# One fetch per set of weights, into the place of its decoded halves; first loads ahead of a branch

## The chip, the cores and the metric

The kernel runs on one core of a Trainium2 chip. The metric is the device time of one launch in microseconds; the median of three runs is taken.

## What is computed

A linear attention with decay is followed by two feed-forward layers. The inputs of the attention are float32; the four weight arrays of the layers are float64 and reach the kernel as their 8-byte words.

```python
state = zeros(B, H, D, D)                       # B 4, H 8, S 768, D 48
for t in range(S):
    cur   = (u * k[t]) outer v[t]
    y[t]  = r[t] @ (state + cur)
    state = w * state + k[t] outer v[t]
x = y as (3072 tokens, 384)
x = max(h, 0.01 * h) @ w_out    with h = x @ w_in     # 384 -> 2048 -> 384
x = (h * cos(h)) @ w_out2       with h = x @ w_in2
```

## The kernel before, in words

The attention is cut into 24 units of 128 tokens (u = 0 to 23, two chunks of 64 tokens each). A unit has three pieces. `prep` (lines 279 to 292) scales its keys, receptances and bonus on VectorE. `piece_a` (line 303) makes the scores `pa` and the state's update `pu` on TensorE, writes the bonus into the diagonal with eight ScalarE copies (line 321), and merges the scores on VectorE (line 322). `piece_y` (`piece_y1` for the first eight units) makes the output `py` on TensorE, copies it out as `yo` on ScalarE (line 371, one buffer), and GpSimd's queue writes it to the DRAM tensor `xt` (line 374). `load_xu` then reads the unit back from `xt` with its rows over partitions, as a quarter of a token block's input `xl` (line 441), and `split_xu` splits it into a rounded high part `xh` (ScalarE, line 445) and the rest `xl` (VectorE, line 446).

The feed-forward layers run over 12 blocks of 512 tokens (0 to 5 for the first layer, 6 to 11 for the second) and, in each, over 16 groups f of 128 hidden columns: a slot (j, f). A slot has nine matmuls for the hidden values (`g1`, line 458: high by low, low by high, high by high, three each), a step on ScalarE and VectorE that applies the nonlinearity and splits the result again (`evac_a`, `evac_b`, lines 463 to 487), and nine matmuls into the block's output (`g2`, lines 498 to 500) two slots later. The slots begin with (0, 0) to (0, 7); then block 0 and block 1 alternate: (0, 8), (1, 0), (0, 9), (1, 1) and so on. Block 0 needs units 0 to 3, block 1 needs units 4 to 7. The pieces of units 4 to 7 are put among the first slots by `due`.

The weights of each f are decoded on the chip from the 8-byte words into a high half `wh` and a low half `wl` (`split_w`, line 256). `load_w` (line 246) fetches the set twice: the words as they are (`wr`), and shifted by two bytes (`wo`), which puts the middle bits of each word into one 32-bit place. Each has two buffers, and so a fetch waits for a decode two sets earlier. A decode has two ScalarE instructions (the sign, line 266; the exponent, line 269) and five on VectorE (lines 267, 270, 271, 273, 275). The tiles `wh10` to `wh15` and `wl10` to `wl15` are first lent to units 0 to 7 (`lent`, line 83) for their inputs and states.

All loads go through SP's queue in the order in which the program lists them, and SP issues them one after the other: one that waits for a buffer holds up all behind it. `load(u)` has five DMAs (lines 112 to 120; keys, receptances, a natural-order copy of r and k, two of v), 1,024 KB together. A branch on the size of the decays (line 189) stands ahead of the loads of unit 1 and later; the path behind it for other decays isn't taken with these inputs. After the branch, the list `first` sets the order on ScalarE and of the loads: `p`, `a` and `y` are pieces of units, `d` a decode, `l` a unit's load. The other engines' orders are made by a planner with a model of the times. For layer 2, sets 0 to 4 have tiles of their own, and set f from 5 on takes the tiles of layer 1's set f - 5 (line 259).

## Time and profile before

| | us |
|---|---|
| median of 3 runs | 957.91 |
| lowest, highest | 955.81, 962.46 |
| span of the profiled execution, first to last instruction | 954.9 |
| TensorE busy with matmuls in the span | 896.4 (94%) |
| VectorE busy | 647.5 (68%) |
| ScalarE busy | 521.7 (55%) |
| bytes moved by DMA | 99.79 MB, of which 84.59 MB read from device memory |

The page of the profile gives the profiled execution's own time as this span; what lies around it in a timed run is the difference to the runs. Busy shares are means over the whole span; the stages differ, and the stages are read from the timelines.

### The profile page before, as it was taken

The numbers are of one execution on the slowest core, as the hardware profiler recorded it, in microseconds if no ns is written. First come the engines' busy times: TensorE is split into PE (matmuls) and PEld (weight loads), VectorE is DVE, ScalarE is ACT, GpSimd is POOL, SyncE is SP. The second block draws the span as 40 slices with busy tenths as digits, with TensorE's granted clock in tenths as the row PEclk, the third lists the DMA queues.
The fourth block names the chain that finished last, engine by engine and source line by source line (L and its number), as shares of the span: only waits on it lengthen the run. The fifth ranks groups of instructions, "written<-read, shape, count | busy, mean of one in ns | idle before, by whom it ended". The sixth has DMA issues, their size and how long they took to land.

```text
span 954.9 us, 15397 instructions
## 1 busy us (share of the span) xinstructions
PE 896.4 (94%) x5954; PEld 734.8 (77%) x5954; DVE 647.5 (68%) x1072; ACT 521.7 (55%) x1050; POOL 53.1 (6%) x92
## 2 busy tenths in 40 slices
PE   1648979999999999999999999999999999999997
PEld 1646858887778888878888788888888888888886
DVE  7768979449865776675848877565665755665654
ACT  1435545635654564563645566665665655665654
POOL 3111100000100000001000000000000000000000
PEclk9957989999999999999999999999999999999999
DMA  7579786024512322252828910100100100100000
GB/s 191 160 248 310 257 287 187 1 68 131 174 47 65 114 98 89 95 204 74 306 69 276 314 72 1 33 34 1 34 34 1 62 4 9 59 1 0 34 1 34
DMA packets 41277, 99.79 MB, mean 104 GB/s; under 512 B 4976, under 2 KB 8176, under 8 KB 41200
## 3 DMA queue, kind: packets, MB, share of 16 engines
q1 hardware_dynamic: 31552, 75.96, 24.6%
q0 software_dynamic: 4896, 14.16, 4.7%
q10 hardware_dynamic: 4752, 8.65, 2.4%
q8 instruction: 47, 0.77, 0.3%
q14 instruction: 30, 0.25, 0.1%
HBM read 84.59 MB, written 14.16 MB: 103 GB/s over the span
## 4 chain that ended last, share of the span: by engine, by line
PE 75%; DMA 10%; DVE 8%; ACT 3%; issue 2%; SPq 0%; POOL 0%; POOLq 0%; ACTq 0%; DVEq 0%
PE ph L458 35%; PE po L498 12%; PE po L499 12%; PE po L500 12%; DMA wr<-in_wmoe 2%; DMA xl<-xt 2%; PE pa L309 2%; PE py L346 2%; ACT ar L321 1%; DMA natt<-in_nat 1%; DMA xt<-yo 1%; PE pu L316 1%; DVE wh L270 1%; DVE wl L275 1%; DMA wo<-in_wmoe 1%
## 5 line engine op out<-in xcount | busy, mean ns | idle before, releaser
L498 PE MATMUL po<-gh,wl 128*128 128x512 f32 x576 | 228.0, 396 | 2.9 <-ACT gh L485 2.7
L499 PE MATMUL po<-gh,wh 128*128 128x512 f32 x576 | 224.6, 390 | 0.0
L500 PE MATMUL po<-gl,wh 128*128 128x512 f32 x576 | 207.0, 391 | 0.7 <-DVE gl L486 0.7
L486 DVE TENSOR_TENSOR gl<-ga,gh 128x512 fp32r<-128x512 f32 x192 | 132.2, 689 | 94.7 <-ACT gh L485 80.6
L485 ACT CAST gh<-ga 128x512 fp32r<-128x512 f32 x192 | 118.6, 619 | 120.1 <-PE po L499 73.3
L458 PE MATMUL ph<-xl,wh 128*128 128x512 f32 x576 | 169.1, 396 | 5.9 <-DVE xl L446 4.8
L458 PE MATMUL ph<-xh,wh 128*128 128x512 f32 x576 | 168.1, 391 | 0.0
L458 PE MATMUL ph<-xh,wl 128*128 128x512 f32 x576 | 165.0, 392 | 0.0
L458 PEld LDWEIGHTS ph<-xl,wh 128*128 128x128 f32 x576 | 108.2, 190 | 30.7 <-DVE xl L446 5.2
L498 PEld LDWEIGHTS po<-gh,wl 128*128 128x128 f32 x576 | 108.1, 188 | 28.0 <-ACT gh L485 4.1
L458 PEld LDWEIGHTS ph<-xh,wl 128*128 128x128 f32 x576 | 109.0, 189 | 23.1
L500 PEld LDWEIGHTS po<-gl,wh 128*128 128x128 f32 x576 | 107.9, 188 | 24.4 <-DVE gl L486 1.8
L458 PEld LDWEIGHTS ph<-xh,wh 128*128 128x128 f32 x576 | 109.0, 189 | 23.0
L499 PEld LDWEIGHTS po<-gh,wh 128*128 128x128 f32 x576 | 108.2, 188 | 21.4
L321 ACT ACTIVATE ar<-ident,bon 64x64 f32<-64x64 f32 (+1 forms) x320 | 80.7, 333 | 26.6 <-DVE bon L290 26.3
L473 DVE SCALAR_TENSOR_TENSOR gt<-gt,ga 128x512 f32<-128x512 f32 x96 | 65.8, 689 | 38.9 <-ACT gt L472 38.4
L468 DVE TENSOR_TENSOR ga<-ph,ga 128x512 f32<-128x512 f32 x96 | 66.0, 688 | 37.8 <-ACT ga L467 37.4
L478 DVE TENSOR_TENSOR ga<-ph,gt 128x512 f32<-128x512 f32 x96 | 65.8, 689 | 36.3 <-ACT gt L477 35.7
L467 ACT ACTIVATE ga<-ph 128x512 f32<-128x512 f32 x96 | 57.1, 594 | 59.2 <-PE ph L458 56.1
L477 ACT ACTIVATE gt<-gt 128x512 f32<-128x512 f32 x96 | 59.8, 627 | 49.8 <-DVE gt L475 49.7
L471 ACT ACTIVATE ga<-ph 128x512 f32<-128x512 f32 x96 | 57.4, 598 | 44.3 <-PE ph L458 30.3
L472 ACT ACTIVATE gt<-ga 128x512 f32<-128x512 f32 x96 | 60.2, 631 | 1.6
(128 smaller groups left out, 754.0 us busy)
## 6 DMA issues: line engine op xcount, KB each, us to landing
wr<-in_wmoe SPq DMA_DIRECT2D x32, 768.0 KB, 6.0
wo<-in_wmoe SPq DMA_DIRECT2D x32, 767.5 KB, 5.7
natt<-in_nat SPq DMA_DIRECT2D x20, 384.0 KB, 4.1
xt<-yo POOLq DMA_DIRECT2D x48, 96.0 KB, 3.6
x2t<-ob ACTq DMA_DIRECT2D x18, 256.0 KB, 2.0
xl<-x2t POOLq DMA_DIRECT2D x6, 768.0 KB, 4.7
kst<-in_ks SPq DMA_DIRECT2D x20, 224.0 KB, 3.4
vs<-in_nat SPq DMA_DIRECT2D x40, 96.0 KB, 4.1
```

The costliest lines, as they stand in the source:

```text
L321: nc.scalar.activation(out=ar[q, c, g], in_=ident2[q], func=AF.Copy, scale=bon[q, g:g + 1])
L458: nc.tensor.matmul(out=p, lhsT=w_[:, 0, k * 128:(k + 1) * 128], rhs=x_[:, k], start=(m == 0), stop=(m == 3 * KT - 1))
L468: nc.vector.tensor_tensor(out=ga, in0=p, in1=ga, op=ALU.max)
L472: nc.scalar.activation(out=gt, in_=ga, func=AF.Copy, bias=MAGIC)
L473: nc.vector.scalar_tensor_tensor(out=gt, in0=gt, scalar=MAGIC, in1=ga, op0=ALU.subtract, op1=ALU.subtract)
L477: nc.scalar.activation(out=gt, in_=gt, func=AF.Sin, scale=-TWOPI)
L478: nc.vector.tensor_tensor(out=ga, in0=p, in1=gt, op=ALU.mult)
L485: nc.scalar.copy(out=gh, in_=ga)
L486: nc.vector.tensor_tensor(out=gl, in0=ga, in1=gh.bitcast(F32), op=ALU.subtract)
L498: nc.tensor.matmul(out=o, lhsT=w_l[:, 1, sl], rhs=gh, start=(f == 0), stop=False)
L499: nc.tensor.matmul(out=o, lhsT=w_h[:, 1, sl], rhs=gh, start=False, stop=False)
L500: nc.tensor.matmul(out=o, lhsT=w_h[:, 1, sl], rhs=gl, start=False, stop=(f == NF - 1))
```

## The change

Each set of weights is fetched once, into a tile that has the size of its two decoded halves and is their place afterwards (tag `w0` to `w15`, and `w16` to `w20` for layer 2's first five). The shifted copy goes; in its place the decode puts the two 16-bit parts of the middle bits side by side in a small tile `mid`: one by a ScalarE copy, the other by VectorE's `and`, now on 16-bit elements. The sign, the masked word and `mid` have tiles of their own (two buffers each). ScalarE has three instructions in a decode, VectorE five.

Since a raw set waits for no decode, the loads are listed anew: ahead of the branch come the loads of units 0 to 3, `uu`, and the sets 0 to 3; sets 4 to 9 and units 4 to 7 stand in `first` (`w` is the fetch of a set); sets 10 to 15, whose places are lent, are fetched after unit 7's `piece_y`. SP's queue is in program order from the start of the kernel.

```diff
--- before.py
+++ after.py
@@ -40,6 +40,7 @@
 HOLD = 16
 AHEAD = 1
 LOADS = 2
+LENT = 10
 EXTRA = 5
 FIRST = 3
 ONE = 8
@@ -48,7 +49,6 @@
 QY = 'gpsimd'
 QO = 'scalar'
 QX = 'gpsimd'
-WRB = 2
 KSB = 2
 NATB = 2
 YOB = 1
@@ -81,11 +81,14 @@
     vs_ = [ap_.tile([128, 2, H, D], F32, name=f"vs{i}") for i in range(2)]
 
     def lent(i, *shape):
-        t = wp.tile([128, 768], F32, tag=i, name=f"lent_{i}")
+        if i[2:] not in lent_:
+            lent_[i[2:]] = wp.tile([128, 2, 768], F32, tag=f"w{i[2:]}", name=f"lent_{i[2:]}")
+        t = lent_[i[2:]]
         n = shape[1] * (shape[2] if len(shape) > 2 else 1)
-        t = t[0:shape[0], 0:n]
+        t = t[0:shape[0], int(i[1] == "l"), 0:n]
         return t.rearrange("p (a b) -> p a b", a=shape[1]) if len(shape) > 2 else t
 
+    lent_ = {}
     ss_ = [lent(i, 128, 768).rearrange("t (c h d) -> t c h d", c=2, h=H) for i in ("wh15", "wl15", "wh10")]
     rf_ = [t[0:PACK, 1] for t in ar_] + [lent(i, PACK, H, HC) for i in ("wh14", "wl14")]
     kf_ = [ap_.tile([PACK, H, HC], F32, tag="ks", bufs=KSB, name="kst") for i in range(2)]
@@ -122,8 +125,28 @@
 
 
     wt = const.tile([PACK, H], F32, name="wt")
+    ub = ap_.tile([128, H, D], F32, name="ub")
+    wh, wl, wraw = {}, {}, {}
+
+    def set_of(L, f):
+        return (wp, f) if L == 0 else (rest[0], NF + f) if f < EXTRA else (wp, f - EXTRA)
+
+    def load_w(L, f):
+        pool, i = set_of(L, f)
+        t = wraw[L, f] = pool.tile([128, 2, 384, 2], I32, tag=f"w{i}", name=f"raw{i}")
+        nc.sync.dma_start(
+            out=t.rearrange("p z a b -> p z (a b)"), in_=wmoe[L, f].bitcast(I32).rearrange("z p c -> p z c"))
+
+    ctx.enter_context(tc.manual_schedule(engines={mybir.EngineType.SP}))
     nc.sync.dma_start(out=wt, in_=wT)
     load(0)
+    nc.sync.dma_start(out=ub, in_=uu)
+    load(1)
+    load(2)
+    load_w(0, 0)
+    load(3)
+    for i in range(1, 4):
+        load_w(0, i)
     w2 = const.tile([PACK, H], F32, name="w2")
     ws = const.tile([PACK, H], F32, name="ws")
     nc.vector.memset(ws, 1.0)
@@ -179,8 +202,6 @@
                 out=ps[TOK[c], i], lhsT=(pw[HALF[0], i] if c else pt[HALF[1], 1, i]),
                 rhs=ident[ROWS[c], ROWS[c]], start=True, stop=True)
     nc.scalar.copy(out=kn, in_=ps)
-    ub = ap_.tile([128, H, D], F32, name="ub")
-    nc.sync.dma_start(out=ub, in_=uu)
     sm = ap_.tile([D, H, D], F32, name="sm")
 
     slow = nc.values_load(flag[0:1, 0:1], min_val=0, max_val=1)
@@ -194,8 +215,8 @@
             t = mp.tile([128, 512], F32, tag=n, bufs=2, name=n)
             return t[:, 0:shape[0] * shape[1]].rearrange("p (a b) -> p a b", a=shape[0])
 
-        buf = [wp.tile([128, 2, 384, 2], I32, tag="wr", bufs=WRB, name="wr") for _ in range(2)]
-        buf = [t.rearrange("p z a b -> p (z a b)").bitcast(F32) for t in buf]
+        buf = [wp.tile([128, 2, 384], I32, tag="dt", bufs=2, name="dt") for _ in range(2)]
+        buf = [t.rearrange("p z a -> p (z a)").bitcast(F32) for t in buf]
         st, cu = [t[:, 0:D * E].rearrange("p (d e) -> p d e", d=D) for t in buf]
         wv, uv = [buf[0][:, D * (E + i):D * (E + i + 1)] for i in range(2)]
         uk = buf[1][:, D * E:D * (E + 1)]
@@ -241,37 +262,26 @@
 
     rebias = const.tile([128, 1], F32, name="rebias")
     nc.vector.memset(rebias, REBIAS)
-    wh, wl, wraw = {}, {}, {}
-
-    def load_w(L, f):
-        t = wp.tile([128, 2, 384, 2], I32, tag="wr", bufs=WRB, name="wr")
-        nc.sync.dma_start(
-            out=t.rearrange("p z a b -> p z (a b)"), in_=wmoe[L, f].bitcast(I32).rearrange("z p c -> p z c"))
-        s = wp.tile([128, 2, 4 * 384], U16, tag="wo", bufs=WRB, name="wo")
-        nc.sync.dma_start(
-            out=s[:, :, 0:4 * 384 - 1],
-            in_=wmoe[L, f].bitcast(U16).rearrange("z p c -> p z c")[:, :, 1:4 * 384])
-        wraw[L, f] = t, s
-
     def split_w(L, f):
-        t, o = wraw.pop((L, f))
-
-        pool, i = (wp, f) if L == 0 else (rest[0], NF + f) if f < EXTRA else (wp, f - EXTRA)
-        h = wh[L, f] = pool.tile([128, 2, 384], F32R, tag=f"wh{i}", name=f"wh{i}")
-        l = wl[L, f] = pool.tile([128, 2, 384], F32R, tag=f"wl{i}", name=f"wl{i}")
+        t = wraw.pop((L, f))
         top = t[:, :, :, 1]
-        mid = o.bitcast(I32).rearrange("p z (c i) -> p z c i", i=2)[:, :, :, 0]
-        s = t[:, :, :, 0].bitcast(F32)
-        a = o.bitcast(I32).rearrange("p z (c i) -> p z c i", i=2)[:, :, :, 1]
+        part = t.rearrange("p z a b -> p z (a b)").bitcast(U16).rearrange("p z (a b) -> p z a b", b=4)
+        a = wp.tile([128, 2, 384], I32, tag="dt", bufs=2, name="dt")
+        s = wp.tile([128, 2, 384], F32, tag="ds", bufs=2, name="ds")
+        mid = wp.tile([128, 2, 384, 2], U16, tag="dm", bufs=2, name="dm")
         nc.scalar.activation(out=s, in_=top.bitcast(F32), func=AF.Sign)
+        nc.vector.tensor_scalar(out=a, in0=top, scalar1=0x7FFFFE00, scalar2=None, op0=ALU.bitwise_and)
+        nc.scalar.copy(out=mid[:, :, :, 0], in_=part[:, :, :, 1])
         nc.vector.tensor_scalar(
-            out=top, in0=top, scalar1=0x7FFFFE00, scalar2=None, op0=ALU.bitwise_and)
-        nc.scalar.activation(out=a, in_=top, func=AF.Relu, scale=8.0, bias=rebias)
+            out=mid[:, :, :, 1], in0=part[:, :, :, 2], scalar1=0x1FF, scalar2=None, op0=ALU.bitwise_and)
+        nc.scalar.activation(out=a, in_=a, func=AF.Relu, scale=8.0, bias=rebias)
+        pool, i = set_of(L, f)
+        hl = pool.tile([128, 2, 2, 384], F32R, tag=f"w{i}", name=f"w{i}")
+        h, l = wh[L, f], wl[L, f] = hl[:, 0], hl[:, 1]
         nc.vector.tensor_tensor(out=h, in0=a.bitcast(F32), in1=s, op=ALU.mult)
         nc.vector.tensor_scalar(
-            out=mid, in0=mid, scalar1=0x1FFFFFF, scalar2=None, op0=ALU.bitwise_and)
-        nc.vector.tensor_scalar(
             out=a, in0=h.bitcast(I32), scalar1=-0x800000, scalar2=None, op0=ALU.bitwise_and)
+        mid = mid.rearrange("p z a b -> p z (a b)").bitcast(I32)
         nc.vector.scalar_tensor_tensor(
             out=l, in0=mid, scalar=2.0 ** -36, in1=a.bitcast(F32), op0=ALU.mult, op1=ALU.mult)
 
@@ -401,6 +411,9 @@
             piece_a(i)
         else:
             piece_y(i)
+            if i == ONE - 1:
+                for f in range(LENT, NF):
+                    load_w(0, f)
             if i + 2 >= ONE:
                 fetch(i + 2)
             if i < 2 * UB:
@@ -530,12 +543,9 @@
         for q in range(FIRST if j == 1 else 0, n):
             due.setdefault(a + (b - a) * q // n, []).append(q)
 
-    ctx.enter_context(tc.manual_schedule(engines={mybir.EngineType.SP}))
     def decode():
         split_w(0, ready[0])
         ready[0] += 1
-        if ready[0] + LOADS - 1 < NF:
-            load_w(0, ready[0] + LOADS - 1)
         if ready[0] >= HOLD:
             while held:
                 load(held.pop(0))
@@ -550,14 +560,10 @@
         ready2[0] += 1
 
 
-    for u in range(1, 4):
-        load(u)
-    for i in range(LOADS):
-        load_w(0, i)
-
-    first = [("p", 0), ("a", 0), ("p", 1), ("a", 1), ("y", 0), ("p", 2), ("a", 2), ("y", 1), ("d", 0),
-             ("p", 3), ("a", 3), ("y", 2), ("l", 4), ("d", 1), ("y", 3), ("l", 5), ("d", 2), ("p", 4)]
-    do = {"p": prep, "a": piece_a, "y": piece_y, "l": load, "d": lambda f: decode()}
+    first = [("p", 0), ("a", 0), ("p", 1), ("a", 1), ("w", 4), ("y", 0), ("l", 4), ("p", 2), ("a", 2), ("w", 5),
+             ("y", 1), ("l", 5), ("d", 0), ("p", 3), ("a", 3), ("w", 6), ("y", 2), ("l", 6), ("w", 7), ("d", 1),
+             ("y", 3), ("l", 7), ("w", 8), ("w", 9), ("d", 2), ("p", 4)]
+    do = {"p": prep, "a": piece_a, "y": piece_y, "l": load, "d": lambda f: decode(), "w": lambda f: load_w(0, f)}
     with tc.manual_schedule(engines={mybir.EngineType.Activation}):
         for k, u in first:
             do[k](u)
@@ -565,8 +571,6 @@
                 load_xu(u)
                 if u:
                     split_xu(u - 1)
-    load(6)
-    load(7)
     npc[0] = ends[0]
     while npc[0] < ends[0] + FIRST:
         do_piece()
```

## Rows read from the trace of the kernel before

**Rows 1.** The page, part 2: busy tenths of the DMA engines in 40 slices.
```profile
DMA  7579786024512322252828910100100100100000
```

**Rows 2.** Timeline of PE: start, us, engine, line, operation, tiles, shape, count, [idle before].
```profile
78.41 1.65 PE L458 MATMUL ph<-xl,wh 128*128 128x512 f32 x3
...
94.41 1.15 PE L309 MATMUL pa<-lent_wh,lent_wh 48*64 48x64 f32 x32
...
96.20 0.50 PE L498 MATMUL po<-gh,wl 128*128 128x512 f32 x1
...
115.25 0.33 PE L363 MATMUL py<-ar,lent_wl 128*64 128x64 f32 x4
...
117.23 0.50 PE L500 MATMUL po<-gl,wh 128*128 128x512 f32 x1
...
137.57 1.65 PE L458 MATMUL ph<-xl,wh 128*128 128x512 f32 x3 [4.76 <-DVE xl L446]
...
141.49 0.85 PE L458 MATMUL ph<-xl,wh 128*128 128x512 f32 x3
```

**Rows 3.** Windows: busy time of each engine in the stretch after the last stall.
```profile
137.57:954.90 817.33, 809.05 (x4782) 661.69 (x4782) 540.43 (x885) 462.98 (x924) 26.19 (x42) 1.00 0.25 81
```

**Rows 4.** Timeline of POOL (its DMA issues), the units' trips through DRAM.
```profile
33.70 1.47 POOL L374 DMA_DIRECT2D xt<-yo  x2 [21.26 <-ACT ar L321]
...
42.09 1.60 POOL L374 DMA_DIRECT2D xt<-yo  x2 [3.34 <-ACT xh L445]
...
63.97 1.27 POOL L374 DMA_DIRECT2D xt<-yo  x2 [4.29 <-ACT wr L266]
...
76.57 1.64 POOL L374 DMA_DIRECT2D xt<-yo  x2 [4.07 <-ACT wr L266]
...
123.10 1.27 POOL L374 DMA_DIRECT2D xt<-yo  x2 [6.72 <-ACT xh L445]
```

**Rows 5.** DMA issues of 33 to 38 us: size each, median us to landing.
```profile
xt<-yo POOLq DMA_DIRECT2D x2, 96.0 KB, 3.1
xl<-xt POOLq DMA_DIRECT2D x1, 192.0 KB, 3.5
```

**Rows 6.** DMA issues of 76.5 to 92 us.
```profile
xt<-yo POOLq DMA_DIRECT2D x2, 96.0 KB, 6.3
...
xl<-xt POOLq DMA_DIRECT2D x1, 192.0 KB, 6.7
```

**Rows 7.** Timeline of SP's queue: when loads are issued.
```profile
10.39 0.34 SPq L112 DMA_DIRECT2D kst<-in_ks  x1
...
78.22 0.65 SPq L112 DMA_DIRECT2D lent_wl<-in_ks  x1
```

**Rows 8.** Windows: PE, PEld, DVE, ACT, POOL busy, granted clock, DMA share, GB/s.
```profile
13.00:18.00 5.00, 1.77 (x32) 1.64 (x30) 2.34 (x4) 0.48 (x1) 0.00 (x0) 1.00 0.97 262
26.00:30.00 4.00, 2.46 (x42) 2.35 (x44) 2.97 (x6) 1.50 (x7) 0.00 (x0) 1.00 1.03 400
...
30.00:40.00 10.00, 8.90 (x238) 8.30 (x235) 8.10 (x14) 3.09 (x10) 2.23 (x3) 1.00 0.32 100
...
50.00:60.00 10.00, 4.16 (x74) 3.76 (x70) 5.83 (x11) 3.01 (x5) 2.27 (x3) 0.67 0.67 206
```

**Rows 9.** Groups by line and form, 0 to 200 us: busy us, mean ns, idle before.
```profile
L266 ACT ACTIVATE wr<-wr 128x768 f32<-128x768 f32 x16 | 14.7, 919 | 12.4 <-DMA wr<-in_wmoe 12.4
...
L271 DVE TENSOR_SCALAR wo<-wo 128x768 int32<-128x768 int32 x16 | 9.2, 575 | 6.2 <-DMA wo<-in_wmoe 6.1
```

**Rows 10.** Timeline of DVE, the stretch before unit 0's first result.
```profile
16.36 0.56 DVE L288 TENSOR_TENSOR natt<-natt,ub 128x384 f32<-128x384 f32 x1 [1.89 <-DMA natt<-in_nat]
...
22.65 0.54 DVE L290 TENSOR_REDUCE bon<-natt 128x8 f32<-128x384 f32 x1
```

**Rows 11.** Timeline of ACT: units 0 and 7 leave PSUM.
```profile
32.80 0.59 ACT L371 COPY yo<-py 112x512 f32<-112x512 f32 x1 [5.30 <-PE py L367]
...
119.18 0.60 ACT L371 COPY yo<-py 112x512 f32<-112x512 f32 x1
```

## Prediction

> **What bounds the kernel now.** I began with the page's slices: the DMA engines are busy through the first seven slices (167 us) and loaded lightly and unevenly after them [rows 1], so a change of fetches can matter there and in few places later. Then TensorE's timeline: the first feed-forward matmul starts at 78.41; from there TensorE has work in hand until it waits 4.76 us for block 1's input, which comes at 137.57 [rows 2]. In the stretch after that it is busy for 809 of 817 us [rows 3]. So the end is set by TensorE, and the question is one number: how early does slot (1, 0) start? Whatever that start gains, the span gains, as long as the stretch behind it stays full. I call it the gate.
>
> What holds the gate before 78.41 is seen on GpSimd's queue. A unit's output is written to DRAM and read back, and the next unit's write is issued only when the read before it has landed: 42.09 is 8.4 us after 33.70, two more trips bring the queue to 63.97, and the next takes 12.6 [rows 4]. A write and a read land in 3.1 and 3.5 us while few loads run [rows 5], and in 6.3 and 6.7 us among many [rows 6]. With the issues and the handover a free trip is 8.4 us; an estimate for one in full traffic, from the same issues, is 0.8 + 6.3 + 0.9 + 6.7 = 14.7 us. Four trips lead to the first slot. Their length hangs on the loads around them, and this change moves just those loads.
>
> **The change part by part.**
>
> *Loads ahead of the branch.* SP issues unit 1's first load at 10.39, behind the branch [rows 7]. Without it the load follows the last one of the head, near 4.6, some 5.8 us earlier. By size and rate (1.05 MB at 262 GB/s for a unit, 0.79 MB at 400 GB/s for a set [rows 8]) a unit's load is 4.0 us of the engines and a set 2.0 us; units 0 to 3 and four sets would be in by about 28 us. VectorE waits 1.89 us for unit 1 ahead of the first bonus result at 22.65 [rows 10], and unit 0's copy from PSUM stands at 32.80 [rows 11]. That the earlier loads are worth is at least this wait and at most the 5.8 us; I take 3.5, as VectorE's own work keeps the order that the planner gave it. Unit 0's copy then comes at 29.3.
>
> *The shifted copy goes.* Sixteen fetches of 2.0 us each go from the first layer, 32 us of traffic, and with them the wait of a fetch for the decode two sets before. Unit 7's load, now issued at 78.22 [rows 7], waits only for unit 3's pieces and comes before the first slot; units 4 to 6 likewise.
>
> *But the loads move into the trips.* From unit 0's copy on, units 4 to 7 and sets 4 to 9 are 4 × 4.0 + 6 × 2.0 = 28 us of traffic, let go step by step as units 0 to 3 finish. I put the four trips at 14.0, 11.0, 10.5 and 8.6, together 44.1, against 42.3 before (33.70 to the last read's landing, 0.6 ahead of the write at 76.57). Bounds are 4 × 8.4 and 4 × 14.7. So the first slot starts 3.5 - 1.8 = **1.7 us** earlier, near 76.7.
>
> *Attention work that no longer stands among the slots.* With their data there early, unit 6's scores and update (94.41 to 96.20) and unit 5's output (as unit 7's, 115.25 to 117.23) can run in TensorE's idle time before the first slot [rows 2]. That is 1.8 + 2.0 = 3.8 us at most, nothing at least; the planner decides, and I take **2.5**.
>
> *The wait at the gate.* The 4.76 us can go, and the slow start behind it: nine matmuls take 3.92 us to 141.49, where three of the next ones take at most 0.85, so 1.4 us are lost [rows 2]. TensorE by itself would reach the gate at 137.57 - 4.76 - 1.7 - 2.5 = 128.6. The other way in is unit 7: copied at 119.18, its write is issued 3.9 us later, behind unit 6's trip, and the gate opens 18.4 us after the copy [rows 2, 4, 11]. With units 5 and 6 through early the 3.9 us shrink to about 0.6; but sets 10 to 15, 12 us of traffic, are now let go by unit 7's output and run beside its trip. A copy at 119.18 - 1.7 - 2.5 = 115.0 and 0.6 + 14.5 behind it (18.4 less 3.9) give 130.1, which is 3.3 us saved at the gate and the slow start kept; if unit 7's pieces come a slot earlier, TensorE is the later one and all 6.2 are saved. I take **4.8**, nearer the second, as nothing holds unit 7's data any more.
>
> *The decode.* ScalarE gets a copy of 768 elements: the sign has the same shape and stride, 919 ns [rows 9]. Three of them come before the first slot, in the shade of the trips (2.8 us if that cover goes), thirteen among the slots, where no row shows ScalarE ending TensorE's wait. Behind the copy on ScalarE waits the exponent step, and VectorE's product waits for that; but the mask on VectorE needs the sign no more, which gives about 0.5 back. VectorE keeps five instructions; the one that becomes 16-bit isn't in the trace. I hold it between 0 and 0.4 us dearer than the 575 ns of its 32-bit form [rows 9], and take 0. Cost at the gate: 0.
>
> *Layer 2.* Its sets from 5 on now wait, before the fetch, for the place that layer 1's last block gives up; they are used a whole block later, some sixteen slots, so a fetch of 2 us and a decode fit. SP has nothing else to issue there. Cost 0, bound 3 us if ScalarE, in order, stands before a set that hasn't landed.
>
> The sum is 1.7 + 2.5 + 4.8 = 9.0. On the profiled execution's span of 954.9 that is 945.9; the median of the runs is 3.0 above that span, so I forecast **948.9 us**. One per cent (9.6 us) is about what a measurement of this kernel can tell from no change.
>
> **The rivals.** *Unit 0 first* (chance 0.25). VectorE may now finish unit 0 before it turns to the others, since the planner sees all loads early; the 22.65 could fall by up to 8 us. The trips start near 25, the first slot near 72, both other terms come in full: 6.4 + 3.8 + 6.2 = 16.4, 941.5 us. For it speaks that VectorE stands idle for loads in this stretch [rows 10]; against it, that the planner mixed the units before as well.
>
> *The gate keeps its distance* (0.22). Unit 7's piece stays at its slot and its trip is as slow as before: the gate then only follows the first slot, 1.7 us earlier, and the time is 956.2. For it: unit 7's write and read lie in the traffic of six sets.
>
> *Full traffic in all trips* (0.12), the one that ends slower. The loads could be let go so evenly that each of four trips costs 14.7: 30.2 + 58.8 + 2.4 = 91.4 for the first slot. Even with units 5 and 6 and unit 7's scores done before it (some 7.6 us off TensorE's list, by the same rows), TensorE reaches the gate at 91.4 + 54.4 - 7.6 = 138.2 (54.4 lie between 78.41 and the wait), and unit 7's trip adds the 4.8 it did before: 143.0, which is 5.4 us late, 963.3. It decides from trips of about 13.4 on average. The row of many loads speaks for it [rows 6]; against it speaks that there are 28 us of traffic for 44 us of trips.
>
> The Trainium skill (SBUF — State Buffer, Door 2's warning in the section "SBUF: two separate sides") holds that a DMA issued by GpSimd stalls while VectorE runs an instruction that takes both ports, since GpSimd can't write the descriptors; by that rule a denser VectorE would lengthen all four trips, whatever the loads, and the time would be this rival's. The rows speak against it as the main cause: between 30 and 40 us VectorE was busy for 8.10 of 10 and the trip was the short one, between 50 and 60 for 5.83, with twice the DMA share, and the trips there were longer (21.9 us for two) [rows 4, 8]. So I give it 0.02 of this rival's 0.12.
>
> **How the numbers follow.** The forecast has 0.41. Of its spread (trips by 3 either way, the two other terms between their ends) a bit over half lies below 948.3. Faster by over 1%: 0.22 of it and nearly all of the first rival, 0.46 together. Slower by over 1%: half of the last rival and 0.03 for a wait in layer 2 or an order that I don't foresee, 0.09. Within 1%: 0.45. The range must leave out 0.2 at most: the first rival's middle and some of its far side give 938, the second rival and the near half of the last give 960.
>
> **What would show it.** Right: unit 1's load near 4.6; no load in the SP queue waiting for VectorE; unit 0's copy near 29; first slot near 77; the wait at the gate below 3 us, at 128 to 131. Wrong: trips of over 13 us up to the first slot, a new wait of TensorE after the gate (sets 10 to 15, or layer 2's sets), or ScalarE as the last to come at a slot.

## The result, and the profile after

| | before | after |
|---|---|---|
| median, us | 960.18 (4 runs, 955.81 to 962.52) | 970.66 (4 runs, 968.52 to 975.43) |
| ratio, 95% interval | | 1.0115 (1.0067 to 1.0163) |
| span of the profiled execution | 954.9 | 970.2 |
| mean granted clock, as a share of full speed | 0.978 | 0.968 |
| bytes moved by DMA | 99.79 MB | 74.63 MB |

The change is slower by about 1.2%, where 948.9 was forecast. (The forecast took 957.91 for the kernel before, the median of three runs; a fourth moves it to 960.18. On the profiled execution's span 945.9 was forecast and 970.2 came.) The traffic did fall by a quarter. The page's DMA slices (24 us each) show where it now lies: full at the start, light in the fourth and fifth slice, nearly full once more in the sixth (121 to 146 us), and idle in the three behind it.

```profile
DMA  9682180004351332131515520010100100100000
```

The windows view (busy time of PE, PEld, DVE, ACT, POOL, then granted clock, DMA share and GB/s) of four stretches: the trips of units 0 and 1, first slot to gate with the wait there, unit 7's trip, and gate to end, which answers to [rows 3].

```profile
30.00:60.00 30.00, 19.90 (x416) 18.15 (x416) 20.36 (x36) 8.81 (x26) 3.25 (x5) 0.68 0.84 242
...
84.74:151.13 66.39, 49.16 (x382) 37.97 (x381) 56.81 (x91) 42.06 (x62) 7.13 (x10) 0.91 0.40 123
...
124.00:140.00 16.00, 13.10 (x56) 9.85 (x54) 10.97 (x17) 11.68 (x16) 2.31 (x3) 1.00 0.98 329
...
151.13:970.20 819.07, 809.47 (x4782) 663.68 (x4782) 527.29 (x862) 471.08 (x933) 26.20 (x42) 0.99 0.18 59
```

TensorE's timeline, the lines that answer to [rows 2]:

```profile
84.74 1.02 PE L471 MATMUL ph<-xl,w 128*128 128x512 f32 x3
...
151.13 1.65 PE L471 MATMUL ph<-xl,w 128*128 128x512 f32 x3 [11.46 <-DVE xl L459]
152.58 2.76 PE L471 MATMUL ph<-xh,w 128*128 128x512 f32 x6
...
160.10 1.65 PE L471 MATMUL ph<-xl,w 128*128 128x512 f32 x3 [2.05 <-DVE ga L481]
```

Set against [rows 2, 3] the 15.3 us of span divide without a rest. The first slot is 6.3 later (84.74 against 78.41). TensorE reaches the gate 54.9 after it (151.13 - 11.46 - 84.74) against 54.4: +0.5. The wait there is 11.46 against 4.76: +6.7. The stretch behind it takes 819.1 against 817.3: +1.7; after the long wait TensorE starts slowly (six matmuls in 2.76 us at 152.58, at a granted clock of 0.50), and a second wait of 2.05 follows.

*The first slot.* GpSimd's queue, beside [rows 4] (`xt<-yo` is a unit's write, `xl<-xt` its read back):

```profile
28.98 1.47 POOL L384 DMA_DIRECT2D xt<-yo  x2 [16.99 <-ACT ar L331]
...
44.52 1.29 POOL L384 DMA_DIRECT2D xt<-yo  x2 [6.63 <-ACT yo L381]
50.86 0.75 POOL L454 DMA_DIRECT2D xl<-xt  x1 [5.05 <-DMA xt<-yo]
60.13 1.27 POOL L384 DMA_DIRECT2D xt<-yo  x2 [8.52 <-ACT xh L458]
68.14 0.76 POOL L454 DMA_DIRECT2D xl<-xt  x1 [6.74 <-DMA xt<-yo]
72.47 1.27 POOL L384 DMA_DIRECT2D xt<-yo  x2 [3.57 <-ACT xh L458]
...
80.99 1.27 POOL L384 DMA_DIRECT2D xt<-yo  x2 [4.15 <-ACT yo L381]
```

Unit 0 is out 4.7 us earlier, and then the trips, from one unit's write to the next one's, take 15.5, 15.6, 12.3 and 8.5, in sum 52.0 against 42.9. Unit 1's read, issued at 50.86, landed 8.7 later; the DMA share of 30 to 60 is 0.84 where before it was 0.49. In the first trip unit 0's read had landed near 41.6 (37.13 and 4.5), and the next write waited until 44.52 for unit 1's output. That delay is VectorE's queue:

```profile
28.69 0.56 DVE L273 TENSOR_SCALAR dt<-raw 128x768 int32<-128x768 int32 x1 [3.93 <-SPq L210]
...
34.16 0.69 DVE L292 TENSOR_TENSOR kst<-kst,pt 112x512 f32<-112x512 f32 x1 [1.71 <-DMA kst<-in_ks]
...
36.84 0.56 DVE L298 TENSOR_TENSOR natt<-natt,ub 128x384 f32<-128x384 f32 x1 [0.92 <-DMA natt<-in_nat]
37.42 0.56 DVE L339 TENSOR_TENSOR lent<-pu,lent 48x384 f32<-48x384 f32 x1
```

Unit 4's preparation waits for its loads, and unit 1's state (the line at 37.42), which TensorE is waiting for, stands behind it. Ahead of that a decode waits 3.93 us for SP (SyncE), which is held at the branch on the decays until 28.57. This second thing looked like a cause; moving the loads back behind the branch did not mend the time (`e2_behind`, below).

*The gate.* GpSimd, then ScalarE:

```profile
124.58 1.27 POOL L384 DMA_DIRECT2D xt<-yo  x2 [4.78 <-ACT yo L381]
131.86 1.04 POOL L454 DMA_DIRECT2D xl<-xt  x1 [6.01 <-DMA xt<-yo]
```

```profile
132.09 0.94 ACT L272 ACTIVATE ds<-raw 128x768 f32<-128x768 f32 x1 [0.98 <-DMA raw<-in_wmoe]
132.91 1.08 ACT L274 COPY dm<-raw 128x768 uint16<-128x768 uint16 x1
...
135.15 0.92 ACT L272 ACTIVATE ds<-raw 128x768 f32<-128x768 f32 x1
...
137.39 0.94 ACT L272 ACTIVATE ds<-raw 128x768 f32<-128x768 f32 x1
...
140.18 0.90 ACT L272 ACTIVATE ds<-raw 128x768 f32<-128x768 f32 x1 [1.03 <-DVE w L281]
...
144.03 0.94 ACT L277 ACTIVATE dt<-dt,rebias 128x768 int32<-128x768 int32 x1 [1.93 <-DVE dt L273]
145.90 1.05 ACT L274 COPY dm<-raw 128x768 uint16<-128x768 uint16 x1 [0.94 <-DVE w L285]
146.82 0.50 ACT L458 CAST xh<-xl 128x384 fp32r<-128x384 f32 x1
```

```profile
150.54 0.53 DVE L459 TENSOR_TENSOR xl<-xl,xh 128x384 fp32r<-128x384 f32 x1
```

Unit 7's read took 7.5 us and landed near 139.4. Its split on ScalarE (the last of ScalarE's lines) ran at 146.82, behind decodes of sets that no slot needed yet, and VectorE's half of it at 150.54. Sets 11 to 15 are fetched at one go, from 123.54 on, behind unit 7's output (set 10 went at 89.72), so they run beside its trip (DMA share 0.98). The planner, which fixes each engine's order when the program is built, put their decodes ahead of its split.

The decode's own prices, groups by line and form up to 200 us (busy us, mean ns of one, idle time before):

```profile
L274 ACT COPY dm<-raw 128x768 uint16<-128x768 uint16 x16 | 16.9, 1063 | 2.2 <-DVE w L285 2.2
...
L272 ACT ACTIVATE ds<-raw 128x768 f32<-128x768 f32 x16 | 14.6, 913 | 2.9 <-DMA raw<-in_wmoe 1.9 <-DVE w L281 1.0
...
L275 DVE TENSOR_SCALAR dm<-raw 128x768 uint16<-128x768 uint16 x16 | 9.8, 610 | 0.0
```

### The profile page after: what moved, and what is told of

It reads as the page before. It is cut to its first block, busy times and chain, and to the rows that moved or that the text cites. A ratio compares the mean times of both kernels' runs of the same rounds, so it can differ in the third digit from the quotient of the medians.

```text
span 970.2 us, 15371 instructions
## 1 busy us (share of the span) xinstructions
PE 901.6 (93%) x5954; PEld 740.5 (76%) x5954; DVE 648.1 (67%) x1072; ACT 548.7 (57%) x1082; POOL 51.7 (5%) x92
## 2 busy tenths in 40 slices
DMA packets 32572, 74.63 MB, mean 77 GB/s; under 512 B 4464, under 2 KB 7664, under 8 KB 32496
## 4 chain that ended last, share of the span: by engine, by line
PE 82%; DMA 6%; DVE 4%; ACT 3%; issue 1%; POOL 0%; SPq 0%; DVEq 0%; POOLq 0%; ACTq 0%
PE ph L471 38%; PE po L511 13%; PE po L512 13%; PE po L513 13%; PE pa L319 2%; DMA raw<-in_wmoe 2%; PE py L356 2%; DMA xt<-yo 1%; PE pu L326 1%; DMA xl<-xt 1%; DMA natt<-in_nat 1%; DVE w L281 1%; ACT ar L331 1%; ACT dm L274 1%; DVE w L285 0%
## 5 line engine op out<-in xcount | busy, mean ns | idle before, releaser
L471 PE MATMUL ph<-xh,w 128*128 128x512 f32 x1152 | 303.6, 392 | 0.0
L471 PEld LDWEIGHTS ph<-xh,w 128*128 128x128 f32 x1152 | 218.4, 190 | 46.0
L511 PE MATMUL po<-gh,w 128*128 128x512 f32 x576 | 227.8, 396 | 3.6 <-ACT gh L498 3.6
L512 PE MATMUL po<-gh,w 128*128 128x512 f32 x576 | 224.9, 390 | 0.0
L513 PE MATMUL po<-gl,w 128*128 128x512 f32 x576 | 208.5, 391 | 0.4 <-DVE gl L499 0.4
L471 PE MATMUL ph<-xl,w 128*128 128x512 f32 x576 | 168.5, 396 | 17.4 <-DVE xl L459 11.5
L471 PEld LDWEIGHTS ph<-xl,w 128*128 128x128 f32 x576 | 108.4, 190 | 41.5 <-DVE xl L459 11.9
L511 PEld LDWEIGHTS po<-gh,w 128*128 128x128 f32 x576 | 108.3, 188 | 28.5 <-ACT gh L498 5.2
L513 PEld LDWEIGHTS po<-gl,w 128*128 128x128 f32 x576 | 107.8, 188 | 23.3 <-DVE gl L499 0.8
L512 PEld LDWEIGHTS po<-gh,w 128*128 128x128 f32 x576 | 108.3, 188 | 21.6
L488 DVE TENSOR_SCALAR gt<-gt 128x512 f32<-128x512 f32 x96 | 40.4, 424 | 1.9
L272 ACT ACTIVATE ds<-raw 128x768 f32<-128x768 f32 x32 | 29.3, 915 | 13.2 <-DMA raw<-in_wmoe 12.1
```

Source lines behind the costliest of these rows:

```text
L471: nc.tensor.matmul(out=p, lhsT=w_[:, 0, k * 128:(k + 1) * 128], rhs=x_[:, k], start=(m == 0), stop=(m == 3 * KT - 1))
L511: nc.tensor.matmul(out=o, lhsT=w_l[:, 1, sl], rhs=gh, start=(f == 0), stop=False)
L512: nc.tensor.matmul(out=o, lhsT=w_h[:, 1, sl], rhs=gh, start=False, stop=False)
L513: nc.tensor.matmul(out=o, lhsT=w_h[:, 1, sl], rhs=gl, start=False, stop=(f == NF - 1))
```

## The experiments

The table has the median in us, the ratio to the kernel before on the same chip, and from the profiled execution the start of the first slot and the sum of TensorE's named waits from 1 us behind that to 200. The profiled execution is one run; in `e4_both`, `f1_two`, `g2_order` and `g3_three` it is 3.7 to 6.6 us under the median, so the ratios decide.

| run | median | ratio (95%) | first slot | waits |
|---|---|---|---|---|
| before | 955 to 960 | 1 | 78.4 | 7.0 |
| after | 970.7 | 1.0115 (1.0067 to 1.0163) | 84.7 | 19.3 |
| e1_gate | 972.1 | 1.0152 (1.0084 to 1.0219) | 82.0 | 16.0 |
| e2_behind | 972.0 | 1.0183 (1.0145 to 1.0222) | 85.8 | 18.3 |
| e4_both | 971.2 | 1.0173 (1.0132 to 1.0215) | 82.5 | 13.0 |
| e3_once | 970.8 | 1.0147 (1.0112 to 1.0182) | 88.7 | 15.5 |
| f1_two | 957.8 | 1.0002 (0.9972 to 1.0032) | 83.0 | 4.1 |
| f3_copy | 961.2 | 1.0026 (0.9999 to 1.0052) | 75.8 | 10.7 |
| f4_head | 956.2 | 0.9991 (0.9960 to 1.0022) | 79.3 | 4.2 |
| f2_paced | 970.6 | 1.0125 (1.0086 to 1.0164) | 83.0 | 14.4 |
| g2_order | 961.2 | 1.0034 (1.0013 to 1.0056) | 82.6 | 6.4 |
| g3_three | 961.5 | 1.0040 (1.0009 to 1.0070) | 78.1 | 7.4 |
| g4_four | 954.8 | 0.9980 (0.9957 to 1.0003) | 76.3 | 8.1 |
| g1_token | 945.9 | 0.9876 (0.9840 to 0.9911) | 74.5 | 2.2 |
| g1_again | 947.2 | 0.9891 (0.9869 to 0.9914) | 73.8 | 2.5 |
| h1_head | 941.7 | 0.9839 (0.9813 to 0.9866) | 70.0 | 0.8 |
| h2_late | 956.2 | 0.9975 (0.9955 to 0.9994) | 85.4 | 4.4 |

**First theory: two places where the order is wrong.** It said: repair the order at the gate, take the loads back behind the branch, and the time returns.

`e1_gate` queues decodes 10 to 15 and the preparations of later units behind the two instructions of unit 7's split (`gate`), on ScalarE and VectorE:

```diff
+            if ready[0] >= LENT:
+                for i in gate:
+                    es.enter_context(tc.issue_after(i.ins))
             split_w(0, ready[0])
```

> The changed kernel with one thing put right: on ScalarE and VectorE the decodes of sets 10 to 15 and the preparations of units 8 and on are queued behind the split of unit 7 (an order, no wait). Theory (the 11.46 us wait at slot (1,0) is the planner's order: unit 7's read landed near 139.4 but its split stood behind five decodes and two preparations): the split runs within 1.5 us of the landing, slot (1,0) starts near 141 in place of 151.1, the wait there falls under 3 us, and the time is 959 to 963 us. Rival 1 (the two engines have too much to do there; work put behind the gate comes back as waits in the slots after it): slot (1,0) early, but TensorE waits 5 us or more between it and 200, and the time is 967 to 971. Rival 2 (the extra ScalarE copy and VectorE operations of the new decode are the loss everywhere): no change, 970 to 972.

`e2_behind` moves the head loads back, and `e4_both` has both edits:

```diff
-    load(1)
-    load(2)
-    load_w(0, 0)
-    load(3)
-    for i in range(1, 4):
-        load_w(0, i)
...
     nc.vector.memset(rebias, REBIAS)
+    load(1)
+    load(2)
+    load_w(0, 0)
+    load(3)
+    for i in range(1, 4):
+        load_w(0, i)
```

> The changed kernel with the loads of units 1 to 3 and of weight sets 0 to 3 moved back behind the branch on the decays; all else stays. Theory (SyncE passes the branch only when what it issued ahead has landed, near 28 us, and VectorE's second decode then waits 3.9 us on SyncE with unit 1 behind it): SyncE is past the branch by 12 us, no VectorE wait on SyncE over 1 us, the trips start as early as before or within 2 us of it (unit 1's first write at 36 to 40 in place of 44.5), the first slot starts at 78 to 80 in place of 84.7, and since the order at slot (1,0) is untouched the time falls by those 5 to 6 us at most: 964 to 968. Rival 1 (not the branch: unit 4's preparation, put ahead in VectorE's order, waits for its loads): the wait of unit 1's state for VectorE stays and the first slot stays at 83 or later, 968 to 972. Rival 2 (unit 0 and 1's loads were worth their 3.5 us, and they are lost too): first slot at 84 or later, 971 to 975.

> The changed kernel with both: head loads behind the branch and unit 7's split ahead of the decodes of sets 10 to 15 and of the preparations of units 8 and on. Theory: the two losses are separate and add up: first slot at 78 to 80, slot (1,0) at 133 to 137, time 952 to 958, under the kernel before's 960. Rival 1 (they hide one another: the gate is then set by unit 7's trip, which has its own length): slot (1,0) at 138 to 141, 958 to 963. Rival 2 (neither is the cause): 968 to 972.

`e3_once` keeps the fetch into the halves' place and the decode, with before's order of loads: units 1 to 3 and two sets behind the branch, then one set issued after each decode.

```diff
     def decode():
         split_w(0, ready[0])
         ready[0] += 1
+        if ready[0] + LOADS - 1 < NF:
+            load_w(0, ready[0] + LOADS - 1)
```

> The single fetch and the new decode alone: order and pace of all loads as in the kernel before (head loads behind the branch, two sets in flight, one more set behind each decode). Theory (fetch and decode cost little, the order of loads is the loss): the first slot starts at 78 to 80, the wait at slot (1,0) is late by the planner's order still (slot (1,0) at 138 to 145), time 956 to 964. Rival (the decode's extra copy on ScalarE and the halves' shared place are the loss): first slot at 81 or later, and ScalarE or VectorE named ahead of TensorE's waits there, time 966 to 972.

All four came out at 971 to 972, in or at the edge of a rival's band and none in the theory's. In the first the split did move: slot (1, 0) began 13.2 us earlier, and most of that was given back behind it (830.8 us from there to the end in place of 819.1):

```profile
137.97 1.65 PE L475 MATMUL ph<-xl,w 128*128 128x512 f32 x3 [4.09 <-DVE xl L463]
...
147.71 0.97 PE L475 MATMUL ph<-xl,w 128*128 128x512 f32 x3 [2.98 <-DVE ga L485]
...
164.16 0.79 PE L515 MATMUL po<-gh,w 128*128 128x512 f32 x1 [4.77 <-ACT gh L502]
```

The 4.77 is an eviction that stands behind the bonus copies of units 8 and 9 and two decodes on ScalarE: the same crowd, one place further on. The second shows that the branch is not it: with the loads behind it, SP issues unit 1's load at 9.62, and the first slot stayed at 85.8. The fourth was the surprise: with before's own order of loads the loss was there in full. So it had to be the decode, or what separates "one set after each decode" from what before really did. Before, a load went into one of two raw buffers, and so waited on the chip until the decode two sets earlier was through with its buffer. In `e3_once` no load waits for a decode: the places of sets 0 to 9 are free from the start, and SP issues sets 5 to 9 one behind the other between 60.01 and 63.5. Set 10 follows at 84.84 and sets 11 to 15 at one go from 121.5, each as soon as the units have given up its place.

**Second theory: the two raw buffers paced the fetches and decodes.** `f1_two` gives the single fetch and the new decode their two raw buffers back, with the loads in before's order (the lines are set against the changed kernel; the sign, too, goes back into the raw buffer):

```diff
 def load_w(L, f):
-        t = wraw[L, f] = pool.tile([128, 2, 384, 2], I32, tag=f"w{i}", name=f"raw{i}")
+        t = wraw[L, f] = wp.tile([128, 2, 384, 2], I32, tag="wr", bufs=WRB, name="wr")
```

> The kernel before with the single fetch and the changed decode (ScalarE's 16-bit copy, VectorE's 16-bit AND), but each raw set goes into one of two raw buffers as before and not into the place of its halves; order of loads as before. The four runs so far, with and without the moved loads, all gave 971 to 972. New theory (the two raw buffers paced the decodes: a set could be fetched and decoded only when one two sets earlier was through, so decodes never stood in front of unit 3's and unit 7's splits or of the evictions): the decodes are paced again, the first slot is at 77 to 80, slot (1,0) at 134 to 138, time 948 to 957, at or under the kernel before. Rival 1 (the copy of 1.05 us a set on ScalarE, 16 sets ahead of 200 us, is the loss): 963 to 971. Rival 2 (something in fetching once, such as a later landing, is the loss): 963 to 971 with a wait on the raw set ahead of the decodes.

Ratio 1.0002: the 13 us are gone. The time is as before and not under it, so without the second fetch nothing was won in this form. In the profiled execution the wait at the gate is gone, and the first slot begins at 83.0, where 77 to 80 was expected. Its trace shows why: ScalarE's half of unit 3's split runs at 76.00, as before (76.38), but VectorE's half only at 80.79 (before 77.28), behind preparations of later units and parts of decodes, with VectorE busy for 12.5 of the 13 us from 70 to 83; and TensorE does attention matmuls up to 83.0 first.

```profile
80.79 0.56 DVE L442 TENSOR_TENSOR xl<-xl,xh 128x384 fp32r<-128x384 f32 x1
```

`f3_copy` prices ScalarE's part alone, in the kernel before:

```diff
+        spare16 = wp.tile([128, 2, 384, 2], U16, tag="sp", bufs=1, name="sp")
+        nc.scalar.copy(
+            out=spare16[:, :, :, 0],
+            in_=t.rearrange("p z a b -> p z (a b)").bitcast(U16).rearrange(
+                "p z (a b) -> p z a b", b=4)[:, :, :, 1])
         nc.scalar.activation(out=s, in_=top.bitcast(F32), func=AF.Sign)
```

> The kernel before (both fetches) with one extra ScalarE copy of 128x768 16-bit values in every decode, its result unread. Theory (the copy is cheap where decodes are paced): 0 to 3 us over the kernel before. Rival (ScalarE's 1.05 us a set delays splits and evictions): 8 to 16 us over it.

0.26%, 2.5 us, with an interval that just reaches none: the copy costs little and is not the loss. `f4_head` is the run with two raw buffers and these lines ahead of the branch (they leave the place behind it):

```diff
+    load(1)
+    load(2)
+    load_w(0, 0)
+    load(3)
+    load_w(0, 1)
```

> As the run with two raw buffers, and the loads of units 1 to 3 and of sets 0 and 1 issued ahead of the branch on the decays. Theory (SyncE holds at the branch until these have landed; with two sets in place of four that is 5 to 6 us earlier than the 28.5 of the changed kernel): SyncE goes on at 20 to 24, unit 0's copy of its output at 28 to 30, and the time is within 3 us of the run with two raw buffers. Rival 1 (the branch's hold is a large loss by itself): 5 us or more over that run, units 4 and 5 late. Rival 2 (the early loads pay their 3.5 us): 2 to 4 us under it.

0.9991: no cost that can be measured. SP, though, went past the branch only at 27.4, not at 20 to 24, and its next load, set 2, waited for its raw buffer until 43.07 in any case. So this run does not price the hold where a load stands ready behind it.

`f2_paced` tried to put the pace into the written order in place of a wait:

```diff
+        with behind(*(gate if ready[0] >= PACED else ()), *(marks[-4] if ready[0] >= LENT else ())):
+            split_w(0, ready[0])
```

> The changed kernel, fetch into the place of the halves kept, paced by order in place of buffers: head loads behind the branch; decodes 5 to 9 queued behind the split of unit 3, decodes 10 to 15 behind the split of unit 7 and the eviction four slots back; preparations and scores of units 8 and on behind the last eviction emitted; sets 12 to 15 fetched on ScalarE's queue behind the split of unit 7, so only two sets are on the way beside unit 7's trip. Theory (bunched decodes and units 8 and 9 pulled ahead are all of the loss): first slot at 78 to 81, slot (1,0) at 131 to 135, no TensorE wait over 1.5 us from there to 200, time 948 to 957. Rival (the order cannot do it, since VectorE has too much work in 80 to 140 whatever the order): slot (1,0) at 136 or later or new waits of 3 us and more before 200, 962 to 972.

970.6, by an error of the edit: sets 8 and 9, too, stood behind unit 7's split, and slot (0, 8) waited 14.4 us for its decode. The run decides nothing on the theory. `g2_order` is without that error: decodes 10 to 15 behind the split and an eviction, sets 12 to 15 fetched behind the split on ScalarE's queue.

```diff
+            if ready[0] >= LENT:
+                for i in gate + marks[-3]:
+                    es.enter_context(tc.issue_after(i.ins))
             split_w(0, ready[0])
...
+                    es.enter_context(tc.issue_after(gate[0].ins))
+                    for i in range(KEEP, NF):
+                        load_w(0, i, nc.scalar)
```

> The run with both repairs (head loads behind the branch, split of unit 7 ahead) with two things more: decodes 10 to 15 also behind the eviction of three slots back, and sets 12 to 15 fetched on ScalarE's queue behind the split of unit 7. Unlike the run paced by order, sets 5 to 9 and the later units' scores are free (there sets 8 and 9 stood behind the split of unit 7 by a slip of the edit, and slot (0,8) waited 14.4 us for its decode). Theory: slot (1,0) at 131 to 136, no wait over 2 us behind it up to 200, time 952 to 959. Rival (an order written at one place only moves the wait on): a wait of 3 us or more between 140 and 300, 962 to 971.

Most of the loss goes (1.0034, from 1.0173 in `e4_both`), and the kernel before is not reached. VectorE's half of unit 7's split runs at 134.0, where the theory put the gate, but a wait of 3.49 us for an eviction follows at 142.47, as the rival said; the first slot keeps its 82.6, which no order at the gate can mend. The time lies between the two bands.

**The test by itself.** `g1_token` is `e3_once` with one line: SyncE stores four bytes of the finished low half of set k ahead of the load of set k + 2. The place, the fetch, the decode and the listed order of the loads stay; the wait is back. The planner's orders of ScalarE and VectorE are made anew with it, and come out different.

```diff
         if ready[0] + LOADS - 1 < NF:
+            nc.sync.dma_start(out=note[:, ready[0] - 1:ready[0]],
+                              in_=wl[0, ready[0] - 1][0:1, 1, 383:384].bitcast(F32))
             load_w(0, ready[0] + LOADS - 1)
```

> The run of the single fetch alone (sets land in the place of their halves, loads in the order of the kernel before, 971) with one line more: ahead of the load of set k+2, SyncE stores four bytes of the finished low half of set k, so that it waits until set k is decoded, as the two raw buffers made it wait. The place, the fetch and the decode stay. Theory (the wait for a free raw buffer is all that was lost): decodes no longer stand ahead of unit 7's split, slot (1,0) at 133 to 138, time 953 to 960. Rival 1 (landing in the halves' place is the loss, for instance sets 10 to 15 waiting for unit 7 to give the place up): 965 to 972. Rival 2 (the small store's own trip of some 2 us per set stalls SyncE): slots wait for decodes, 961 to 966.

> The run with the four-byte store once more, beside the two above on one chip: 943 to 948, ratio to the kernel before 0.984 to 0.991. If the 1.2 per cent was an accident of one chip, 0.995 or more.

945.9, and 947.2 on another chip: 25 us under `e3_once` and 1.1 to 1.2% under the kernel before, better than its theory asked. Windows of `e3_once` and, below it, of `g1_token`; then SP's queue, GpSimd's queue and ScalarE of `g1_token`:

```profile
30.00:60.00 30.00, 20.37 (x467) 18.76 (x463) 22.68 (x41) 14.02 (x38) 5.53 (x8) 0.83 0.68 199
```

```profile
30.00:60.00 30.00, 18.70 (x444) 17.54 (x442) 18.43 (x33) 12.15 (x28) 6.28 (x9) 0.80 0.35 102
124.00:140.00 16.00, 16.00 (x72) 13.08 (x71) 14.98 (x25) 12.61 (x19) 0.00 (x0) 1.00 0.31 100
```

```profile
48.60 0.29 SPq L542 DMA_DIRECT2D note<-w  x1
48.94 0.38 SPq L137 DMA_DIRECT2D raw<-in_wmoe  x1
```

```profile
35.20 1.47 POOL L377 DMA_DIRECT2D xt<-yo  x2 [22.77 <-ACT ar L324]
...
42.93 1.29 POOL L377 DMA_DIRECT2D xt<-yo  x2 [3.10 <-ACT xh L448]
...
49.98 1.27 POOL L377 DMA_DIRECT2D xt<-yo  x2 [2.62 <-ACT xh L448]
...
73.24 1.27 POOL L377 DMA_DIRECT2D xt<-yo  x2 [4.78 <-ACT xh L448]
...
117.00 1.27 POOL L377 DMA_DIRECT2D xt<-yo  x2 [3.90 <-ACT yo L374]
121.13 0.75 POOL L444 DMA_DIRECT2D xl<-xt  x1 [2.86 <-DMA xt<-yo]
```

```profile
123.16 0.93 ACT L265 ACTIVATE ds<-raw 128x768 f32<-128x768 f32 x1
123.97 1.10 ACT L267 COPY dm<-raw 128x768 uint16<-128x768 uint16 x1
124.90 0.53 ACT L448 CAST xh<-xl 128x384 fp32r<-128x384 f32 x1
```

Both places are healed by the one wait. Between the two profiled executions lie 26.9 us: the first slot is 14.2 earlier (74.5 for 88.7), and the waits behind it are 13.3 less. SP issues the load 0.3 us after the store, so the store's own trip holds nothing up. The DMA share of 30 to 60 falls from 0.68 in `e3_once` to 0.35, and the four trips from 47.4 us (33.42 to 80.78) to 38.0. Unit 7 takes 7.9 us from write to split (14.8 to the landing alone, and 22.2 to the split, in the changed kernel; 13.3 to the split before), with a part of one decode ahead of it. TensorE has 2.2 us of named waits behind the first slot.

The wait acts in two ways, and the runs do not separate them: fewer fetches run beside the trips, and fewer decodes stand in ScalarE's order ahead of the splits. Counted by the sign instructions in the timelines, 7 decodes begin ahead of unit 3's split and 16 ahead of unit 7's in `e3_once` (6 and 16 in the changed kernel, 5 and 13 before), and 4 and 11 in `g1_token`. By the order at the gate alone `e1_gate` got nothing back; `g2_order`, which also fetched four sets later, got most of the loss back, with its first slot still at 82.6.

The dose: `g4_four` lets four sets be on the way (the store of set k ahead of set k + 4), `g3_three` is `f1_two` with three raw buffers and three sets.

```diff
-LOADS = 2
+LOADS = 4
```

```diff
-LOADS = 2
+LOADS = 3
...
-WRB = 2
+WRB = 3
```

> As the run with the four-byte store, but four sets on the way in place of two (the load of set k+4 waits for set k). Theory by dose: between that run and the unpaced 971, at 959 to 967, with two decodes more ahead of unit 7's split. Rival (only the unlimited case hurts): within 2 us of that run.

> The run with two raw buffers (958), with three of them and three sets on the way. Theory by dose (each set more on the way lets one decode more stand ahead of a split, 3.0 us on ScalarE and 3.6 on VectorE): slot (1,0) 0 to 4 us later, time 957 to 963. Rival (any depth with a buffer of its own is as good): 956 to 959. Rival 2 (deeper is better): 951 to 955.

In place: 0.988 to 0.989 with two, 0.998 with four, 1.015 with no limit. The run with four came out at 954.8, under the 959 to 967 of its theory and over the rival's band, so the dose was smaller than expected: 6 decodes begin ahead of unit 3's split there and 15 ahead of unit 7's, but its first slot, at 76.3, is only 1.8 later. With raw buffers: 1.000 with two, 1.004 with three, the intervals overlapping. The first series shows that more sets on the way cost more; the second goes the same way without showing it.

**The two places apart, and the early loads.** `h2_late` paces only the last sets in the changed kernel, by the same store (the loads of sets 12 to 15 wait); `h1_head` is `g1_token` with the five lines of `f4_head`. The diff is the first one's.

```diff
-                for f in range(LENT, NF):
+                for f in range(LENT, LENT + 2):
                     load_w(0, f)
...
+        if LENT < ready[0] < NF - 1:
+            nc.sync.dma_start(out=note[:, ready[0] - 1:ready[0]],
+                              in_=wl[0, ready[0] - 1][0:1, 1, 383:384].bitcast(F32))
+            load_w(0, ready[0] + 1)
```

> The changed kernel as it stands, loads of units and of sets 0 to 9 untouched, with sets 10 to 15 alone paced: 10 and 11 behind unit 7's output as now, and each later one behind the four-byte store of the set two before it. Theory (the loss has two places, the first slot and slot (1,0), and this repairs the second): first slot at 83 to 86 as in the changed kernel, the wait at slot (1,0) under 3 us, time 85 + 869 and 2 to 4 us of waits, 955 to 959. Rival (work put off comes back as waits behind slot (1,0), as when only the order was repaired there): 963 to 971.

> The run with the four-byte store (two sets on the way, in the place of their halves, 945.9), and the loads of units 1 to 3 and of sets 0 and 1 issued ahead of the branch on the decays, as the changed kernel has them. In that run the first slot began at 74.52 and TensorE was busy from there to the end (943.5 less 74.5 is 869.0), so the time should follow the first slot. Theory (the prediction's step: unit 0's copy some 3.5 us earlier, and 1.8 us of it lost in the trips): first slot at 71 to 73.5, time 1 to 3 us under that run. Rival (SyncE's hold at the branch makes units 4 and 5 late, or a split behind a decode): first slot at 75 or later, 0 to 6 us over it.

`h2_late`: first slot at 85.4 as in the changed kernel, waits 4.4, time 956.2: pacing these four loads takes off 1.4%, all of it in the waits, and the late first slot remains. `h1_head`: 941.7, the best of all, 5.5 us under `g1_again` on the same chip where its theory asked for 1 to 3, its first slot 3.8 earlier:

```profile
70.02 1.65 PE L467 MATMUL ph<-xl,w 128*128 128x512 f32 x3 [1.43 <-DVE xl L455]
```

## Why the prediction was wrong

*Step by step.* The head start was right: unit 1's load is issued at 4.65 (4.6), unit 0's copy stands at 28.08 (29.3). The decode was right at no cost that is clear of the noise: 1,063 ns for ScalarE's copy (919 taken), 610 for the 16-bit mask (between 575 and 975 allowed), and `f3_copy` at 1.0026 with an interval from 0.9999. Layer 2 was right: gate to end 819.1 against 817.3, of which the slow start and the wait of 2.05 are a part.

The trips were mis-sized: 44.1 forecast, from the first write to the last landing 50.1 (28.98 to 79.1). The first slot came at 84.7 for 76.7: 6.0 of that are the trips, 3.2 the split of unit 3, which ran 2.5 us after the landing with VectorE's half behind other work, less 1.2 of head start. The rival of full traffic had this mechanism, for two of the trips and not for four.

The attention work that was to come before the first slot (2.5) did so in part, and gave nothing: 382 matmuls stand between slot and gate in place of 467, but the time is 54.9 against 54.4. TensorE idles for 5.8 us there in place of 1.9. Its longest wait, 3.2 at 93.69, is for the nonlinearity of an early slot, which stood on VectorE behind instructions of decodes.

The step that failed is in one clause. Under "The shifted copy goes" the prediction lists, as a thing that goes, "the wait of a fetch for the decode two sets before", and at the gate it argues that "nothing holds unit 7's data any more". It priced the wait as a cost. The runs show that the wait kept fetches out of the units' trips and decodes out of the splits' way: one line that puts it back is worth 25 us (`e3_once` to `g1_token`, the planner's order following it). At the gate the prediction had 15.1 us from unit 7's copy to the slot; the copy came at 123.70 and the slot 27.4 later. The data were there near 139.4, and the split then stood behind decodes for 7.4 us on ScalarE and 3.2 more on VectorE, a wait that was in no rival.

What was right and hidden: the early loads are worth what they promised once the decodes are paced. Unit 0's copy goes from 34.15 in `g1_again` to 30.33 in `h1_head`, and all of it arrives at the first slot, 73.8 to 70.0, as the four trips do not get longer (38.1 us from 31.23 to 69.33, for 38.0 in `g1_token`). The forecast of 948.9 lies between the changed kernel and that version, but by other terms.

*The rule from the Trainium skill* (SBUF — State Buffer, section "SBUF: two separate sides"), by which VectorE instructions that take both ports stall a DMA issued by GpSimd, isn't needed for these trips. From 30 to 60 us VectorE was busy for 20.4 us in the changed kernel and 18.4 in `g1_token`, with DMA shares of 0.84 and 0.35; the reads of units 0 and 1 landed in 4.5 and 8.7 us in the one and 2.8 in the median in the other. The reads' times go with the traffic. No run varied VectorE alone, so the rule is not excluded either.

*What stays open.* Why pacing through the halves' place (0.988) beats pacing through two raw buffers (1.000) by 12 us: the first slots differ by 8.5 us (74.5 and 83.0). Two things differ with them, and no run tells them apart. The wait is not quite the same: SP waits for VectorE's last instruction of a decode with the store, and with the raw buffers only for the product two instructions earlier. And the planner's order differs: 5 and 14 decodes begin ahead of the splits of units 3 and 7 in `f1_two`, 4 and 11 in `g1_token`. And `f4_head` began its first slot 3.7 us earlier than `f1_two` for 1.6 us that lie inside the intervals.

## What to carry to other kernels

A wait on a free buffer is also a throttle. Before a change takes one away, ask what it held back: which transfers will now run beside a short, serial round trip, and which work, now ready earlier, will be queued ahead of the late arrival that TensorE waits for. If a buffer is to go, keep its wait: here a four-byte store per set, which makes the queue wait for the decode two sets back, turned the +1.5% of `e3_once` into -1.2%, and into -1.6% together with the early loads.

Repairing the order at the one place where TensorE waits may only move the wait on, as in `e1_gate`; look at the sum of the waits over the whole stretch, and at what feeds the crowd. And where a planner makes the engines' orders, a one-line edit changes more than its line: compare the orders in the traces before calling two runs alike.

## What the runs showed of the hardware

SP went past the branch on the decays only when the loads that it had issued ahead of it had landed: in the changed kernel it issues the last of them at 17.73, which takes 10.3 us to land, and the next load at 28.57, with the DMA engines idle from about 27.

```profile
17.73 0.37 SPq L137 DMA_DIRECT2D raw<-in_wmoe  x1
...
28.57 0.38 SPq L137 DMA_DIRECT2D raw<-in_wmoe  x1
```

So loads moved ahead of this branch also hold up the loads behind it. In `f4_head` and `h1_head` SP's waits at the branch end at 27.4 and 26.0, but what stands next in its queue waits for a decode until 43.07 and 45.26; that the hold cost nothing is shown for such a queue only.

The same hold is seen on another engine: VectorE's mask of set 1 is listed with 3.93 us of waiting for SP itself at 28.69, though that set was issued before the branch.
